# One fixed load order, a transpose moved to DMA, a gate sum in one VectorE pass and a paired epilogue in a gated sequence mixer

## The chip, the cores and the metric

The kernel runs on one NeuronCore of one Trainium2 chip. The metric is the device time of one execution in microseconds (us). The span of the profile is about 2 us shorter than that time (215.2 us against 217.1 us in the profiled run of the kernel before). Runs of one kernel mostly agree within 0.3%, but now and then one is far slower; such runs are marked slow and are compared with nothing.

Engine names in the profile: PE is TensorE (matmuls), PEld its weight loads, DVE is VectorE, ACT is ScalarE, POOL is GpSimd, SP is the engine that issues the DMAs, PEclk the clock that TensorE was granted, as a share of full speed.

## The reference

The inputs are bf16, sequence 2048, width 640, hidden width 1536.

```python
x = A_q
g = _sigmoid((x * gate_w).sum(-1, keepdims=True))
a = _A_ref(x, A_k, A_v, A_shift_k, A_ssm_k, A_ssm_D)
b = _B_ref(x, B_w1, B_b1, B_w2, B_b2)
return g * a + (1 - g) * b

def _A_ref(q, k, v, shift_k, ssm_k, ssm_D):
    # [cut] k_shift: a causal convolution of k along the sequence with 4 taps per channel
    kv = k_shift * v
    # [cut] y: a causal convolution of kv along the sequence with ssm_k (2048 taps per channel),
    #       written with a real FFT of length 4096
    y = y + kv * ssm_D[None, None, :]
    return q * y

def _B_ref(x, w1, b1, w2, b2):
    h = _layernorm(x, axis=-1)
    u = jnp.einsum("bsd,sf->bdf", h, w1) + b1             # mixes along the sequence
    u = _gelu(u)                                          # the tanh approximation
    y = jnp.einsum("bdf,fs->bds", u, w2) + b2
    return (lambda x, *d: x.transpose(*d))(y, 0, 2, 1)
```

## The kernel before

The long convolution is done in a frequency domain that is split into four interleaved parts. The names that the profile shows:

- **ssm → wT → C_82, C_83**: ssm_k is loaded, transposed on TensorE (ScalarE evicts it as wT; to evict is to copy a result from PSUM, into which TensorE writes, to SBUF, the on-chip working memory), and multiplied with the table FTB of cosines and sines ("W-forward", 128 matmuls). ScalarE evicts the result as C_82 (first half of the sequence) and C_83 (second half). VectorE then combines the four parts with two-input passes ("mixing", which also writes SS).
- **KT, DG → ksh → vkv, kv**: k is loaded transposed. The 4-tap convolution is 35 matmuls per 512 rows with DG, a set of diagonal matrices that GpSimd builds from shift_k (shk). ScalarE evicts ksh, VectorE multiplies it by v: vkv (first half), kv (second half).
- **vkv, kv with FTB → C_84, C_85**: the "A-forward", twice 64 matmuls. Then VectorE multiplies the spectra, and the inverse uses GTB, the transpose of FTB.
- **X, ring → GT → O**: x is loaded as X; layer-norm statistics (bn_stats, bn_aggr) and normalisation on VectorE; m1 (w1 in two buffers "ring", 384 matmuls); gelu on ScalarE; m2 (w2 as W_0 and W_1, 384 matmuls). None of this needs the convolution, so m1 and m2 serve as filler for TensorE.
- **gate**: the sum of x · gate_w (loaded as gwb) per row goes into gpre, tanh gives gth, and small GpSimd passes give g, 1 - g and (1 - g) · b2.

A list scheduler inside the kernel places all operations with estimated durations before anything runs. The outcome is one fixed order per engine, and each engine then works in that order: an operation whose input is late holds up everything behind it on its engine.

These are the parts that the change and the argument touch:

```python
        ssm_load(0)
        x_load(0)
        ssm_load(1)
        dma(Drow[:, :], dr(A_ssm_D, 0, [[0, 1], [1, D]]), 1280)
        dma(shk[:, :, :], dr(A_shift_k, 0, [[4, 128], [512, ND], [1, 4]]), 5120, noncontig=True)
        dma(gwb[:, :], dr(gate_w, 0, [[0, 128], [1, D]]), 128 * 1280)
        x_load(1)
        ssm_load(2)
        ssm_load(3)
        x_load(2)
        x_load(3)
        # [cut] b1, b2
        for db in range(ND):
            kT_load(0, db)
        # [cut] then, in the text, v 0/1, k second half, v 2/3, and both w1 blocks last

        def ln_apply(hk):
            # [cut]
            tt("DVE", xg[:, :, :], X[:, hk, :, :], V(gwb, 0, [[0, 4], [1, D]]), ALU.mult)
            for p in range(4):
                act(xg[:, p, :], xg[:, p, :], ACT.Copy, acc=gpre[:, 4 * hk + p:4 * hk + p + 1], name="ga")
            ts("POOL", vtmp[:, r], mv[:, r, 1], 1e-5, None, ALU.add)
            tt("POOL", rstd[:, r], vtmp[:, r], V(cst, 1, [[0, 4]]), ALU.pow)
            for p in range(4):
                # normalise X in place with mv and rstd [cut]

        tt("POOL", DG[:, :, :, :].rearrange("p a b c -> p (a b) c"),
           V(ident, 0, [[0, 20], [1, 128]]), V(shk, 0, [[1, 20], [0, 128]]), ALU.mult)
        # [cut] cast of b1 (b1f) on GpSimd
        act(gth[:, :], gpre[:, :], ACT.Tanh, scale=0.5)

        # GTB: FTB block by block through TensorE, evicted by ScalarE
        for g in range(8):
            # [cut]
            mms(vt, items, name="gtr", prio=10 ** 6 + 20 + p)
            act(GTB[:, p, :, :, :, :].rearrange("p a b c d -> p (a b c d)"), lambda s: s[:, :], ACT.Copy, vt=vt, name="gte")
```

Of the kernel before, what the change touches and what calls it, by code (L numbers as in the profile page):

```python
# [13 lines left out]
ALU = mybir.AluOpType  # L14
# [292 lines left out]
class _Op:  # L307
    __slots__ = ("eng", "dur", "emit", "prio", "idx", "ndep", "succ", "vt", "vtrole", "end", "start", "kind", "lat", "deps", "name")
# [12 lines left out]
class _Sched:  # L321
# [3 lines left out]
    def __init__(self, T, slots):  # L325
        self.T = T
        self.slots = slots
        self.ops = []
        self.hist = {}
        self.limit = {"mlp": 2}  # L330
# [20 lines left out]
    def add(self, eng, dur, emit, reads, writes, prio=None, vt=None, lat=0.0, name=""):  # L351
# [21 lines left out]
        op.deps = deps  # L373
        self._rec(op, reads, "R")
# [4 lines left out]
    def run(self):  # L379
        ops = self.ops  # L380
        for op in ops:
            op.succ = []
            op.ndep = len(op.deps)
        for op in ops:
            for d in op.deps:
                d.succ.append(op)
        engs = list(ENGS) + ["SP", "QA"]
# [18 lines left out]
        while started < n:  # L406
# [6 lines left out]
            for e in engs:  # L413
# [42 lines left out]
                if op.vt is not None:  # L456
                    op.vt.left -= 1
                    if op.vt.left == 0:
                        heapq.heappush(frees, (op.end + 0.05, op.vt.slot, op.vt.cls))
                for s in op.succ:  # L460
# [36 lines left out]
def _build(nc, A_q, A_k, A_v, A_shift_k, A_ssm_k, A_ssm_D, B_x, B_w1, B_b1, B_w2, B_b2, gate_w, out):  # L497
# [8 lines left out]
    with ExitStack() as es:  # L506
# [72 lines left out]
        xg = alloc("xg", [128, 4, D], BF16, at=base_of(GT))  # L579
# [6 lines left out]
        cgb = [alloc(f"cgb{i}", [128, D], BF16, at=base_of(FTB) + 1280 * i) for i in range(6)]  # L586
# [19 lines left out]
        def ts(eng, o, a, s1, s2, op0, op1=None, mode=1, prio=None):  # L606
            n = n_of(o)
            d = dve_dur(n, mode) if eng == "DVE" else n / 900.0 + 0.3
# [44 lines left out]
        def mms(vt, items, prio=None, name="mm"):  # L653
            dur = sum(max(n_of(r), 64) for _, _, r, _, _ in items) / 2400.0
# [10 lines left out]
        ndma = [0]  # L665

        def dma(o, i, nbytes, stream="SP", prio=None, sem=None, rate=230.0, **kw):
# [5 lines left out]
            return SC.add(stream, nbytes / rate / 1000.0, lambda s: T.dma(stream, o, i, sem, **kw), [i], [o], prio=prio, lat=-1.0, name="dma")  # L673
# [13 lines left out]
        def ssm_load(hk):  # L687
            dma(ssm[:, :, 512 * hk:512 * hk + 512], dr(A_ssm_k, 512 * hk, [[S, 128], [128 * S, ND], [1, 512]]), 128 * ND * 1024)

        def x_load(hk):  # L690
            dma(X[:, hk, :, :], dr(A_q, 512 * hk * D, [[4 * D, 128], [1, 4 * D]]), 128 * 5120)

        def w1_load(c, hk):
            dma(ring[c % 2][:, 4 * hk:4 * hk + 4, :], dr(B_w1, 512 * hk * F + 512 * c, [[4 * F, 128], [F, 4], [1, 512]]), 128 * 4096)

        def kT_load(h, db):
            dma(KT[h][:, db, 16:1040], A_k[0, 1024 * h:1024 * h + 1024, db * 128:db * 128 + 128], 128 * 2048, rate=170.0, transpose=True)

        def v_load(hk):
            dst = vkv0[:, hk, :, :] if hk < 2 else v1[:, hk - 2, :, :]  # L700
            dma(dst, dr(A_v, 512 * hk * D, [[4 * D, 128], [1, 4 * D]]), 128 * 5120)
# [4 lines left out]
        dma(Drow[:, :], dr(A_ssm_D, 0, [[0, 1], [1, D]]), 1280)  # L706
        dma(shk[:, :, :], dr(A_shift_k, 0, [[4, 128], [512, ND], [1, 4]]), 5120, noncontig=True)
        dma(gwb[:, :], dr(gate_w, 0, [[0, 128], [1, D]]), 128 * 1280)
        x_load(1)
        ssm_load(2)  # L710
        ssm_load(3)
        x_load(2)
        x_load(3)
        dma(b1t[:, :], dr(B_b1, 0, [[1, 128], [128, FT]]), 3072, noncontig=True)
        dma(b2t[:, :].rearrange("p (a b) -> p a b", a=4), dr(B_b2, 0, [[4, 128], [512, 4], [1, 4]]), 4096, noncontig=True)
# [12 lines left out]
        for p in PORD:  # L728
            pv = pint[:, p, :, 1, :]
            tt("DVE", pv, V(acol, p, [[4, 2], [0, 256]]), V(brow, 0, [[0, 2], [1, 256]]), ALU.mult, mode=1)  # L730
            ts("DVE", pint[:, p, :, 0, :], pv, 1024.0, None, ALU.add)
            pa = pint[:, p, :, :, :].rearrange("q a b c -> q (a b c)")
            ts("DVE", pa, pa, 4095, None, ALU.bitwise_and)
# [3 lines left out]
        def transp(h, p, kt):  # L737
            vt = _VT("t")
# [12 lines left out]
        def fwd(src, h, p, dst, slot, scale, name):  # L751
            for k2 in range(2):
                for c in range(2):
                    vt = _VT("f")
# [9 lines left out]
        def mixing(R, Th, Ts):  # L764
# [5 lines left out]
            tt("DVE", sl(Th, Ts), sl(R, 0), sl(R, 2), ALU.add)  # L770
            tt("DVE", sl(R, 0), sl(R, 0), sl(R, 2), ALU.subtract)
# [291 lines left out]
```

## Time and profile before

The median is 217.5 us. What matters in the profile:

| reading | value |
|---|---|
| TensorE busy | 192.9 us, 90% of the span |
| VectorE busy / ScalarE busy | 184.5 us / 119.3 us |
| end of the second A-forward | 98.1 us |
| unbroken TensorE work from | 72.95 us to 211.6 us |
| C_83 evictions end; products vkv start at | 51.0 us; 61.2 and 64.0 us |

The head of the page (busy time; then busy tenths in 40 slices of 5.4 us):

```profile
PE 192.9 (90%) x1406; PEld 139.7 (65%) x1406; DVE 184.5 (86%) x197; ACT 119.3 (55%) x181; POOL 18.0 (8%) x22
PE   0579944999879899999999999999999999999993
ACT  2798999799984996395213112113314472323751
PEclk9999995599999999999999999999999999999998
```

TensorE has gaps in the first third only, and two slices there were run at half clock (0.50 from 33.3 to 43.0 us). From the chain that ended last (start in us, duration in us, what):

```profile
19.96 9.05 ACT C_82 L641 x15
29.02 2.81 ACT xg L641 x8
34.20 2.94 ACT xg L641 x8
43.77 7.27 ACT C_83 L641 x12
51.04 2.83 ACT xg L641 x8
55.70 2.87 ACT xg L641 x8
72.95 138.65 PE pp L291 x1022
```

Until about 60 us ScalarE paces: its evictions, with the gate sums (xg) among them. After 73 us only TensorE counts, at 138.65 / 1022 = 0.136 us per matmul.

### The profile page before, as it was taken

Reading aid. Unit: us, or ns where it says so; the run is one execution under the profiler, and the core shown is the slowest. Engines: PE = TensorE matmul, PEld = TensorE weight load, DVE = VectorE, ACT = ScalarE, POOL = GpSimd, SP = SyncE. Lnnn points to the kernel's source line nnn. Section 1 sums busy time; section 2 is a strip of 40 time slices with the busy share of each in tenths; the row PEclk is TensorE's granted clock in tenths of the full one; section 3 lists DMA queues with packets and bytes.
Section 4 is the critical chain, followed back from the end, with each engine's and each line's share of the span. In section 5 each row is a group of like instructions: output and inputs, shape, how many; then the busy total and the mean of one; then the engine's idle time right before and its main releaser. Section 6 shows DMA issues by size and latency. Waiting matters only on the chain.

```text
span 215.2 us, 3363 instructions
## 1 busy us (share of the span) xinstructions
PE 192.9 (90%) x1406; PEld 139.7 (65%) x1406; DVE 184.5 (86%) x197; ACT 119.3 (55%) x181; POOL 18.0 (8%) x22
## 2 busy tenths in 40 slices
PE   0579944999879899999999999999999999999993
PEld 0456523556547557766777777778887778887672
DVE  8999599998999258966999999999997669998650
ACT  2798999799984996395213112113314472323751
POOL 1262215004060000000000000000000000000000
PEclk9999995599999999999999999999999999999998
DMA  5997999999100000000480095077070098000131
GB/s 182 355 375 149 143 176 215 349 353 412 64 0 3 0 0 3 0 0 3 128 262 3 3 318 215 3 237 299 28 265 2 3 276 261 4 0 0 61 125 62
DMA packets 32721, 28.71 MB, mean 133 GB/s; under 512 B 14145, under 2 KB 31170, under 8 KB 32706
## 3 DMA queue, kind: packets, MB, share of 16 engines
q1 hardware_dynamic: 32706, 28.49, 43.7%
q8 instruction: 11, 0.18, 0.4%
q14 instruction: 4, 0.03, 0.0%
HBM read 23.25 MB, written 2.62 MB: 120 GB/s over the span
## 4 chain that ended last, share of the span: by engine, by line
PE 72%; ACT 23%; DMA 2%; issue 0%; DVE 0%
PE pp L291 72%; ACT xg L641 5%; ACT C_82 L641 4%; ACT C_83 L641 3%; ACT wT L641 3%; DMA ssm<-in_A_ssm_k_dram 2%; ACT FTB L641 2%; ACT L641 2%; ACT ksh_94 L641 2%; ACT GTB L641 1%; ACT C_84 L641 1%; ACT ksh_95 L641 0%; ACT O_100 L641 0%; ACT GT L641 0%; DVE O_100 L603 0%
## 5 line engine op out<-in xcount | busy, mean ns | idle before, releaser
L291 PE MATMUL pp<-X,ring_80 128*128 128x320 bf16 x256 | 35.6, 299 | 1.5 <-ACT ksh_95 L641 1.5
L641 ACT ACTIVATE O_100<-pp,c_66,omg 128x640 bf16<-128x640 f32 x16 | 14.2, 885 | 35.0 <-PE pp L291 35.0
L291 PEld LDWEIGHTS pp<-X,ring_80 128*128 128x128 bf16 x256 | 24.9, 98 | 11.5 <-issue 1.8
L641 ACT ACTIVATE GT<-pp,b1f 128x640 bf16<-128x640 f32 x12 | 9.5, 793 | 38.1 <-PE pp L291 38.0
L291 PE MATMUL pp<-GT,W_1_99 128*128 128x320 bf16 x192 | 26.9, 299 | 0.0
L291 PE MATMUL pp<-GT,W_0_98 128*128 128x320 bf16 x192 | 26.4, 299 | 0.0
L291 PEld LDWEIGHTS pp<-GT,W_1_99 128*128 128x128 bf16 x192 | 21.7, 113 | 4.4
L291 PEld LDWEIGHTS pp<-GT,W_0_98 128*128 128x128 bf16 x192 | 21.8, 113 | 4.3
L291 PE MATMUL pp<-wT,FTB 128*128 128x320 bf16 x128 | 21.8, 335 | 0.0
L291 PE MATMUL pp<-ident,ssm 128*128 128x128 bf16 x80 | 9.5, 287 | 12.9 <-ACT wT L641 6.8
L291 PEld LDWEIGHTS pp<-wT,FTB 128*128 128x128 bf16 x128 | 12.4, 109 | 9.0 <-ACT C_82 L641 1.9
L291 PE MATMUL pp<-X,ring_81 128*128 128x320 bf16 x128 | 17.7, 299 | 0.0
L291 PEld LDWEIGHTS pp<-ident,ssm 128*128 128x128 bf16 x80 | 7.1, 136 | 15.1 <-ACT wT L641 8.0
L291 PEld LDWEIGHTS pp<-X,ring_81 128*128 128x128 bf16 x128 | 12.5, 98 | 4.8
L790 DVE BATCH_NORM_STATS2 stats<-X 128x6 f32<-128x320 bf16 x32 | 13.5, 461 | 0.0
L641 ACT ACTIVATE wT<-pp 128x640 bf16<-128x640 f32 x16 | 10.1, 740 | 4.5 <-PE pp L291 4.5
L603 DVE TENSOR_TENSOR C_83<-C_84 128x2560 bf16<-128x2560 bf16 x4 | 5.9, 1490 | 7.2 <-ACT C_84 L641 7.2
L641 ACT ACTIVATE xg<-xg 128x640 bf16<-128x640 bf16 x16 | 11.8, 804 | 0.0
L641 ACT ACTIVATE C_83<-pp 128x640 bf16<-128x640 f32 x16 | 10.1, 746 | 1.5 <-PE pp L291 1.5
L603 DVE TENSOR_TENSOR C_84<-C_85 128x2560 bf16<-128x2560 bf16 x5 | 7.4, 1490 | 3.8 <-ACT C_85 L641 3.8
L603 DVE TENSOR_TENSOR C_85<-C_85 128x2560 bf16<-128x2560 bf16 (+1 forms) x6 | 10.3, 1710 | 0.1
L291 PE MATMUL pp<-vkv_91,FTB 128*128 128x320 bf16 x64 | 9.7, 301 | 0.6 <-ACT GT L641 0.6
(116 smaller groups left out, 335.1 us busy)
## 6 DMA issues: line engine op xcount, KB each, us to landing
ring_80<-in_B_w_dram SPq DMA_DIRECT2D x8, 512.0 KB, 6.0
W_0_98<-in_B_w_dram SPq DMA_DIRECT2D x4, 768.0 KB, 5.8
W_1_99<-in_B_w_dram SPq DMA_DIRECT2D x4, 768.0 KB, 5.3
ssm<-in_A_ssm_k_dram SPq DMA_DIRECT2D x4, 640.0 KB, 8.5
X<-in_A_q_dram SPq DMA_DIRECT2D x4, 640.0 KB, 8.9
out_dram<-O_100 SPq DMA_DIRECT2D x16, 160.0 KB, 2.1
ring_81<-in_B_w_dram SPq DMA_DIRECT2D x4, 512.0 KB, 8.6
vkv_91<-in_A_v_dram SPq DMA_DIRECT2D x2, 640.0 KB, 10.1
```

What stands on the lines that cost most here:

```text
L291: ins = self.nc.tensor.matmul(ps_ap, lhsT=lhsT, rhs=rhs, start=start, stop=stop, skip_group_check=True)
L603: return SC.add(eng, d, lambda s: T.op(eng, lambda e: e.tensor_tensor(o, a, b, op), [a, b], [o]), [a, b], [o], prio=prio, name="tt")
L641: return T.op("ACT", lambda e: e.activation(o, src, func, **kw), rr + [src], ww)
L790: SC.add("DVE", 0.42, (lambda o, i: lambda s: T.op("DVE", lambda e: e.bn_stats(o, i), [i], [o]))(o, i), [i], [o])
```

## The change

The change has four parts. The loads are issued in one fixed order (first ssm_k and x, then the small tables, the first w1 block, k, v, the second w1 block, the rest of k and v), so that TensorE has m1 matmuls early. GTB is made by DMA transposes instead of TensorE and ScalarE. The gate sum is one VectorE pass per tile, with accumulation, instead of a product on VectorE and 16 sums on ScalarE. The epilogue works on pairs of tiles, with 8 stores instead of 16. Beside these, some durations in the scheduler's model are corrected, PSUM buffers are shared out to the stages in another way, and the mixing uses wider passes in three of its four places.

```diff
-        dma(shk[:, :, :], dr(A_shift_k, 0, [[4, 128], [512, ND], [1, 4]]), 5120, noncontig=True)
-        dma(gwb[:, :], dr(gate_w, 0, [[0, 128], [1, D]]), 128 * 1280)
-        x_load(1)
+        dma(gwb[:, :], dr(gate_w, 0, [[0, 128], [1, D]]), 128 * 1280, chain=True)
+        for hk in range(1, 4):
+            x_load(hk)
         ssm_load(2)
         ssm_load(3)
-        x_load(2)
-        x_load(3)
+        dma(shk[:, :, :], dr(A_shift_k, 0, [[4, 128], [512, ND], [1, 4]]), 5120, noncontig=True, chain=True)
+        # [cut] b1, b2
+        for hk in range(4):
+            w1_load(0, hk)
         for db in range(ND):
             kT_load(0, db)
# [cut] every load gets chain=True: it may not be issued before the one written ahead of it
+            stt("DVE", junk[1][:, :], xs, 1.0, gwb[:, :], ALU.mult, ALU.mult, acc=gpre[:, t:t + 1])
-            tt("DVE", xg[:, :, :], X[:, hk, :, :], V(gwb, 0, [[0, 4], [1, D]]), ALU.mult)
-            for p in range(4):
-                act(xg[:, p, :], xg[:, p, :], ACT.Copy, acc=gpre[:, 4 * hk + p:4 * hk + p + 1], name="ga")
-        for g in range(8):
-            # [cut] TensorE transposes and ScalarE evictions of GTB
+        for p in range(4):
+            dma(GTB[:, p, :, :, :, :].rearrange("q a b c d -> q (a b c) d"), FTB[:, p, :, :, :, :].rearrange("q a b c d -> q (a b c) d"), 128 * 2048, rate=200.0, transpose=True, prio=10 ** 5)
# inverse, per pair of tiles:
-                    tt("DVE", cg[:, :], cg[:, :], qv, ALU.mult)
-                    tt("DVE", O1[:, hk, p, :], cg[:, :], O1[:, hk, p, :], ALU.add)
-                    dma(dr(out, (512 * hk + p) * D, [[4 * D, 128], [1, D]]), O1[:, hk, p, :], 128 * 1280, sem="out")
+                tt("DVE", cg[:, :, :], cg[:, :, :], (q_lo if h == 0 else q_hi)[:, :, p, :], ALU.mult)
+                tt("DVE", ov, cg[:, :, :], ov, ALU.add)
+                dma(dr(out, (1024 * h + p) * D, [[4 * D, 128], [512 * D, 2], [1, D]]), ov, 256 * 1280, sem="out")
# [cut] model durations, PSUM slot classes, wider mixing passes
```

More of the change, by code (lines that the diff above doesn't have):

```diff
@@ L307 @@
 class _Op:
-    __slots__ = ("eng", "dur", "emit", "prio", "idx", "ndep", "succ", "vt", "vtrole", "end", "start", "kind", "lat", "deps", "name")
+    __slots__ = ("eng", "dur", "emit", "prio", "idx", "ndep", "succ", "vt", "vtrole", "end", "start", "kind", "lat", "deps", "name", "after", "nafter", "asucc")
 class _VT:
@@ L329, in __init__ @@
         self.hist = {}
-        self.limit = {"mlp": 2}
+        self.limit = {"mlp": 2, "cv": 3}
     def _conf(self, op, aps, mode, deps):
@@ L373, in add @@
         op.deps = deps
+        op.after = set()
         self._rec(op, reads, "R")
@@ L382, in run @@
             op.succ = []
-            op.ndep = len(op.deps)
+            op.asucc = []
+            op.ndep = len(op.deps) + len(op.after)
         for op in ops:
@@ L386, in run @@
                 d.succ.append(op)
+            for d in op.after:
+                d.asucc.append(op)
         engs = list(ENGS) + ["SP", "QA"]
@@ L459, in run @@
                         heapq.heappush(frees, (op.end + 0.05, op.vt.slot, op.vt.cls))
+                for s in op.asucc:
+                    avail[s] = max(avail[s], op.start)
+                    s.ndep -= 1
+                    if s.ndep == 0:
+                        heapq.heappush(pend[s.eng], (avail[s], s.prio, s.idx))
                 for s in op.succ:
@@ L578, in _build @@
         ksh = [alloc(f"ksh{i}", [128, 4, D], BF16, at=base_of(GT) + 5120 * (1 + i)) for i in range(2)]
-        xg = alloc("xg", [128, 4, D], BF16, at=base_of(GT))
         pint = alloc("pint", [128, 4, 2, 2, 256], I32, at=base_of(ring[1]))
@@ L585, in _build @@
         q_hi = alloc("q_hi", [128, 2, 4, D], BF16, at=base_of(C[0]))
-        cgb = [alloc(f"cgb{i}", [128, D], BF16, at=base_of(FTB) + 1280 * i) for i in range(6)]
+        cgb = [alloc(f"cgb{i}", [128, 2, D], BF16, at=base_of(FTB) + 2560 * i) for i in range(3)]
         def n_of(ap):
@@ L604, in tt, with ts @@
                           [a, b], [o], prio=prio, name="tt")
-        def ts(eng, o, a, s1, s2, op0, op1=None, mode=1, prio=None):
+        def ts(eng, o, a, s1, s2, op0, op1=None, mode=1, prio=None, extra=0.0):
             n = n_of(o)
-            d = dve_dur(n, mode) if eng == "DVE" else n / 900.0 + 0.3
+            d = dve_dur(n, mode) + extra if eng == "DVE" else n / 900.0 + 0.3
             rr = [a] + [x for x in (s1, s2) if isinstance(x, bass.AP)]
@@ L653, in mms @@
         def mms(vt, items, prio=None, name="mm"):
-            dur = sum(max(n_of(r), 64) for _, _, r, _, _ in items) / 2400.0
+            dur = sum(max(n_of(r) / 2400.0, 0.117) for _, _, r, _, _ in items)
             rd = []
@@ L665, in _build, with dma @@
         ndma = [0]
-        def dma(o, i, nbytes, stream="SP", prio=None, sem=None, rate=230.0, **kw):
+        last = [None]
+        def dma(o, i, nbytes, stream="SP", prio=None, sem=None, rate=280.0, chain=False, **kw):
             if sem is None:
@@ L672, in dma @@
                 T.add_dma_sem(sem, es.enter_context(nc.semaphore(f"s_{sem}")))
-            return SC.add(stream, nbytes / rate / 1000.0, lambda s: T.dma(stream, o, i, sem, **kw), [i], [o], prio=prio, lat=-1.0, name="dma")
+            o_ = SC.add(stream, nbytes / rate / 1000.0, lambda s: T.dma(stream, o, i, sem, **kw), [i], [o], prio=prio, lat=-1.0, name="dma")
+            if chain:
+                if last[0] is not None:
+                    o_.after.add(last[0])
+                last[0] = o_
+            return o_
         def dr(t, off, ap):
@@ L687, in ssm_load, with after @@
         def ssm_load(hk):
-            dma(ssm[:, :, 512 * hk:512 * hk + 512], dr(A_ssm_k, 512 * hk, [[S, 128], [128 * S, ND], [1, 512]]), 128 * ND * 1024)
+            dma(ssm[:, :, 512 * hk:512 * hk + 512], dr(A_ssm_k, 512 * hk, [[S, 128], [128 * S, ND], [1, 512]]), 128 * ND * 1024, chain=True)
         def x_load(hk):
-            dma(X[:, hk, :, :], dr(A_q, 512 * hk * D, [[4 * D, 128], [1, 4 * D]]), 128 * 5120)
+            dma(X[:, hk, :, :], dr(A_q, 512 * hk * D, [[4 * D, 128], [1, 4 * D]]), 128 * 5120, chain=True)
         def w1_load(c, hk):
-            dma(ring[c % 2][:, 4 * hk:4 * hk + 4, :], dr(B_w1, 512 * hk * F + 512 * c, [[4 * F, 128], [F, 4], [1, 512]]), 128 * 4096)
+            dma(ring[c % 2][:, 4 * hk:4 * hk + 4, :], dr(B_w1, 512 * hk * F + 512 * c, [[4 * F, 128], [F, 4], [1, 512]]), 128 * 4096, chain=True)
         def kT_load(h, db):
-            dma(KT[h][:, db, 16:1040], A_k[0, 1024 * h:1024 * h + 1024, db * 128:db * 128 + 128], 128 * 2048, rate=170.0, transpose=True)
+            dma(KT[h][:, db, 16:1040], A_k[0, 1024 * h:1024 * h + 1024, db * 128:db * 128 + 128], 128 * 2048, rate=170.0, transpose=True, chain=True)
         def v_load(hk):
             dst = vkv0[:, hk, :, :] if hk < 2 else v1[:, hk - 2, :, :]
-            dma(dst, dr(A_v, 512 * hk * D, [[4 * D, 128], [1, 4 * D]]), 128 * 5120)
+            dma(dst, dr(A_v, 512 * hk * D, [[4 * D, 128], [1, 4 * D]]), 128 * 5120, chain=True)
+        def after(o_, *prev):
+            o_.after.update(prev)
+            return o_
         ssm_load(0)
@@ L705, in _build @@
         ssm_load(1)
-        dma(Drow[:, :], dr(A_ssm_D, 0, [[0, 1], [1, D]]), 1280)
-        dma(shk[:, :, :], dr(A_shift_k, 0, [[4, 128], [512, ND], [1, 4]]), 5120, noncontig=True)
-        dma(gwb[:, :], dr(gate_w, 0, [[0, 128], [1, D]]), 128 * 1280)
-        x_load(1)
+        dma(Drow[:, :], dr(A_ssm_D, 0, [[0, 1], [1, D]]), 1280, chain=True)
+        dma(gwb[:, :], dr(gate_w, 0, [[0, 128], [1, D]]), 128 * 1280, chain=True)
+        for hk in range(1, 4):
+            x_load(hk)
         ssm_load(2)
         ssm_load(3)
-        x_load(2)
-        x_load(3)
-        dma(b1t[:, :], dr(B_b1, 0, [[1, 128], [128, FT]]), 3072, noncontig=True)
-        dma(b2t[:, :].rearrange("p (a b) -> p a b", a=4), dr(B_b2, 0, [[4, 128], [512, 4], [1, 4]]), 4096, noncontig=True)
+        dma(shk[:, :, :], dr(A_shift_k, 0, [[4, 128], [512, ND], [1, 4]]), 5120, noncontig=True, chain=True)
+        dma(b1t[:, :], dr(B_b1, 0, [[1, 128], [128, FT]]), 3072, noncontig=True, chain=True)
+        dma(b2t[:, :].rearrange("p (a b) -> p a b", a=4), dr(B_b2, 0, [[4, 128], [512, 4], [1, 4]]), 4096, noncontig=True, chain=True)
+        for hk in range(4):
+            w1_load(0, hk)
         for db in range(ND):
@@ L730, in _build @@
             tt("DVE", pv, V(acol, p, [[4, 2], [0, 256]]), V(brow, 0, [[0, 2], [1, 256]]), ALU.mult, mode=1)
-            ts("DVE", pint[:, p, :, 0, :], pv, 1024.0, None, ALU.add)
+            ts("DVE", pint[:, p, :, 0, :], pv, 1024.0, None, ALU.add, mode=2)
             pa = pint[:, p, :, :, :].rearrange("q a b c -> q (a b c)")
-            ts("DVE", pa, pa, 4095, None, ALU.bitwise_and)
+            ts("DVE", pa, pa, 4095, None, ALU.bitwise_and, mode=2)
             act(FTB[:, p, :, :, :, :].rearrange("q a b c d -> q (a b c d)"), pa, ACT.Sin, bias=cst[:, 0:1],
@@ L737, in transp @@
         def transp(h, p, kt):
-            vt = _VT("t")
+            vt = _VT("cv")
             items = []
@@ L753, in fwd @@
                 for c in range(2):
-                    vt = _VT("f")
+                    vt = _VT("cv")
                     items = []
@@ L762, in fwd, with mixing @@
                     act(o, two, ACT.Copy, vt=vt, name=name + "e", **kw)
-        def mixing(R, Th, Ts):
+        def mixing(R, Th, Ts, fine=False):
             def sl(h, s, n=1):
@@ L769, in pr @@
                 return V(h, s * SL + (1280 if rev else 0), [[-1280 if rev else 1280, 2], [1, 1280]])
-            tt("DVE", sl(Th, Ts), sl(R, 0), sl(R, 2), ALU.add)
-            tt("DVE", sl(R, 0), sl(R, 0), sl(R, 2), ALU.subtract)
-            tt("DVE", sl(Th, Ts + 1), sl(R, 1), sl(R, 3), ALU.add)
-            tt("DVE", sl(R, 1), sl(R, 1), sl(R, 3), ALU.subtract)
+            for i, n in (((0, 1), (1, 1)) if fine else ((0, 2),)):
+                tt("DVE", sl(Th, Ts + i, n), sl(R, i, n), sl(R, 2 + i, n), ALU.add)
+                tt("DVE", sl(R, i, n), sl(R, i, n), sl(R, 2 + i, n), ALU.subtract)
             tt("DVE", sl(R, 2), sl(Th, Ts), sl(Th, Ts + 1), ALU.add)
@@ L789, in ln_tile @@
                     o, i = stats[:, t, 6 * ci:6 * ci + 6], xs[:, 320 * ci:320 * ci + 320]
-                    SC.add("DVE", 0.42, (lambda o, i: lambda s: T.op("DVE", lambda e: e.bn_stats(o, i), [i], [o]))(o, i), [i], [o])
+                    SC.add("DVE", 0.46, (lambda o, i: lambda s: T.op("DVE", lambda e: e.bn_stats(o, i), [i], [o]))(o, i), [i], [o])
                 o, i = mv[:, t, :], stats[:, t, :]
                 SC.add("DVE", 0.2, (lambda o, i: lambda s: T.op("DVE", lambda e: e.bn_aggr(o, i), [i], [o]))(o, i), [i], [o])
+            stt("DVE", junk[1][:, :], xs, 1.0, gwb[:, :], ALU.mult, ALU.mult, acc=gpre[:, t:t + 1])
         def ln_apply(hk):
@@ L806, in ln_apply @@
                 t = 4 * hk + p
-                ts("DVE", X[:, hk, p, :], X[:, hk, p, :], mv[:, t, 0:1], rstd[:, t:t + 1], ALU.subtract, ALU.mult, mode=4)
+                ts("DVE", X[:, hk, p, :], X[:, hk, p, :], mv[:, t, 0:1], rstd[:, t:t + 1], ALU.subtract, ALU.mult, mode=4, extra=0.17)
         srcW = lambda h: (lambda kt, p, ci: wT[:, 2 * h + kt, p, 320 * ci:320 * ci + 320])
@@ L820, in _build @@
             if h == 0:
-                mixing(C[0], SS, 0)
+                mixing(C[0], SS, 0, fine=True)
             else:
@@ L834, in _build @@
             v_load(hk)
+        for hk in range(4):
+            w1_load(1, hk)
         for db in range(ND):
@@ L838, in _build @@
             v_load(hk)
-        for hk in range(4):
-            w1_load(0, hk)
-        for hk in range(4):
-            w1_load(1, hk)
         def v1mix(Wh, Ws, Vh, Vs):
@@ L857, in kv @@
             for d0, nb in ((0, 2), (2, 2), (4, 1)):
-                vt = _VT("k")
+                vt = _VT("cv")
                 items = []
@@ L909, in w2_load @@
                 dma(W2[hk % 2][:, 6 * a:6 * a + 6, :], dr(B_w2, a * 6 * 128 * S + 512 * hk, [[S, 128], [128 * S, 6], [1, 512]]), 128 * 6144)
-        for g in range(8):
-            vt = _VT("g")
-            items = []
-            for b in range(8 // 2):
-                pass
-            p, kt = g // 2, g % 2
-            if kt == 0:
-                continue
-            for b in range(8):
-                kt_, c_, k2_ = b // 4, (b // 2) % 2, b % 2
-                items.append(((lambda s, b=b: s[:, 128 * b:128 * b + 128]), FTB[:, p, kt_, c_, k2_, :], ident[:, :], True, True))
-            mms(vt, items, name="gtr", prio=10 ** 6 + 20 + p)
-            act(GTB[:, p, :, :, :, :].rearrange("p a b c d -> p (a b c d)"), lambda s: s[:, :], ACT.Copy, vt=vt, name="gte")
+        for p in range(4):
+            dma(GTB[:, p, :, :, :, :].rearrange("q a b c d -> q (a b c) d"), FTB[:, p, :, :, :, :].rearrange("q a b c d -> q (a b c) d"), 128 * 2048, rate=200.0, transpose=True, prio=10 ** 5)
         HORD = (2, 3, 0, 1)
@@ L993, in inverse @@
                 hz, sz = Z[p]
+                cg = cgb[ncg[0] % len(cgb)]
+                ncg[0] += 1
                 for kt in range(2):
-                    hk = 2 * h + kt
-                    t = 4 * hk + p
-                    vt = _VT("i")
+                    t = 8 * h + 4 * kt + p
+                    vt = _VT("cv")
                     items = []
@@ L1004, in inverse @@
                     mms(vt, items, name="inv")
-                    cg = cgb[ncg[0] % len(cgb)]
-                    ncg[0] += 1
-                    act(cg[:, :].rearrange("p (a b) -> p a b", a=2), two, ACT.Copy, scale=gg[:, t:t + 1], vt=vt, name="cg")
-                    qv = (q_lo if h == 0 else q_hi)[:, kt, p, :]
-                    tt("DVE", cg[:, :], cg[:, :], qv, ALU.mult)
-                    tt("DVE", O1[:, hk, p, :], cg[:, :], O1[:, hk, p, :], ALU.add)
-                    dma(dr(out, (512 * hk + p) * D, [[4 * D, 128], [1, D]]), O1[:, hk, p, :], 128 * 1280, sem="out")
+                    act(cg[:, kt, :].rearrange("p (a b) -> p a b", a=2), two, ACT.Copy, scale=gg[:, t:t + 1], vt=vt, name="cg")
+                ov = O1[:, 2 * h:2 * h + 2, p, :]
+                tt("DVE", cg[:, :, :], cg[:, :, :], (q_lo if h == 0 else q_hi)[:, :, p, :], ALU.mult)
+                tt("DVE", ov, cg[:, :, :], ov, ALU.add)
+                dma(dr(out, (1024 * h + p) * D, [[4 * D, 128], [512 * D, 2], [1, D]]), ov, 256 * 1280, sem="out")
         ncg = [0]
```

## The prediction

> **What bounds the kernel now.** The span is 215.2 us, PE busy 192.9 us (page, part 1). The chain of waits ends in 138.65 us of unbroken PE from 72.95 us on: 1022 matmuls, 135.7 ns each; only removing matmuls helps there. The loss lies before: in the stretch table PE is busy about 46 us of the first 73, and in slices 7 and 8 of the page the granted clock is 0.5. The chain there is ACT: C_82 evictions 9.05 us (0.60 each), two rounds of "xg" (29 to 38 us, PE busy 3.1 of 9.0), C_83, two more rounds of xg inside the ksh evictions (51 to 59 us).
>
> **Removed.** ACT: 16 xg passes, 0.72 us apart (four rows of the chain, 11.5 us, all before 59 us); 4 GTB evictions (4.0 us); one table load (1.28 us). PE: 32 FTB transposes (3.7 us). DVE: 4 xg products (8.9 us).
>
> **Added.** DVE: 16 scalar_tensor_tensor passes. batch_norm_stats of 320 columns starts every 0.42 us, so 640 columns[...] is an estimated 0.75 us: 12 us. DMA: 4 transposes of 256 KB. The ten k transposes took about 20 us together (DMA saturated, 145 GB/s), so about 8 us, between the k and v loads.[...]
>
> **Moved.** First w1 block ahead of the k transposes: PE gets MLP matmuls as filler by about 24 us instead of 61.6. ACT stays the pacer early: wT of half 0 done near 14 us (18.7 before), C_82 near 24 (29.0), C_83 near 38 (51.0). Then kv is PE work (0.90 us per 7 matmuls), and vkv waits on DVE: 13 statistics tiles of 1.7 us, the first mixing (11 us), and v, landed near 43 us; the A-forward starts near 50 us (68.4 before, really 73). The second A-forward finishes about 91 us (98 before).
>
> **The sum.** From there 768 matmuls x 135.7 ns = 104 us. DVE needs about 64 us to the first inverse tile, PE about 67, so DVE is just hidden. The tail grows from 1.4 to about 2.5 us before the last output DMA: one eviction, two 1280-wide DVE passes. About 91 + 104 + 5 = 200 us span, plus the 2.3 us between span and time: 202 us, 7% faster.
>
> The half clock should vanish.[...] the filler should prevent it. Worth about 3 us, within the sum.
>
> **What would show it.** Granted clock 0.9 or more throughout; no xg in ACT; C_83 evictions ending at 36 to 41 us; unbroken PE from 50 to 60 us; DVE near 100% busy until 60 us; no PE wait for GTB.
>
> **What would make it wrong.** SBUF-to-SBUF transposes much slower than those from DRAM hold back v in the same queue: up to 5 to 8 us. scalar_tensor_tensor slower than 0.75 us: each 0.1 us is 1.6 us on DVE.[...] tanh (needing all 16 gate sums) and the first gelu (needing the last normalised X) can block evictions: 1 to 3 us. More filler than I assume: 196 us.
>
> Predicted 202 us, range 196 to 209; faster 0.95, same 0.04, slower 0.01.

The sum came to 91 + 104 + 5 us of span and 2.3 us more, 202 us. The 0.75 us of a gate pass, within the 91, is the author's estimate; the trace shows the 0.42 us of a pass over 320 columns, and twice that would be 0.84. That the filler would prevent the half clock, worth about 3 us within the sum, was the author's estimate too.

## More of the kernel before

The lines of the timeline give start, duration, engine, line, operation, out<-in, size.

```profile
9.67 4.46 POOL L603 TENSOR_TENSOR DG<-ident,shk 128x2560 bf16<-128x2560 bf16 x1 [8.07 <-DMA shk<-in_A_shift_k_dram]
11.04 4.43 DVE L603 TENSOR_TENSOR xg<-X,gwb 128x2560 bf16<-128x2560 bf16 x1
32.64 1.48 DVE L603 TENSOR_TENSOR xg<-X,gwb 128x2560 bf16<-128x2560 bf16 x1
```

The same VectorE product takes 1.48 us alone and 4.43 us beside GpSimd's DG product.

## The result, and the profile after

The median after is 210.11 us (209.94 to 210.69, four runs). The ratio to the kernel before is 0.967, with a 95% interval of 0.964 to 0.970: 3.3% faster. Ratios here are the mean time of one kernel's fast runs over that of the other's of the same rounds, so they are not quite the ratio of the medians quoted. The prediction said 202 us and at most 209: the direction was right, about half of the gain did not come.

The head of the page, after:

```profile
PE 187.9 (90%) x1370; PEld 136.5 (65%) x1374; DVE 189.8 (91%) x203; ACT 104.3 (50%) x144; POOL 19.7 (9%) x22
PE   0699947999987899999999999999999999999990
ACT  4989960886378964586211112122313264413571
PEclk9999995899999999999999999999999999999999
```

ScalarE lost 15.0 us of work, TensorE 5.0 us; VectorE gained 5.3 us. Parts of the chain that ended last, after:

```profile
20.16 4.83 DVE junk_75 L629 x2
28.41 1.35 POOL vtmp L621
29.77 1.37 POOL b1f L843
31.13 1.02 POOL rstd L611
61.13 1.28 ACT L649
67.79 1.28 ACT L649
79.84 123.62 PE pp L291 x909
203.49 0.80 ACT cgb_105 L649
```

No xg is left, and ScalarE is no longer the early pacer; VectorE and the small GpSimd passes that feed it are. The two rows of 1.28 us on ScalarE are table loads, for tanh at 61 us and for gelu at 68 us. The timeline after, VectorE and GpSimd around 20 us and 28 to 34 us:

```profile
19.33 0.83 DVE L808 BATCH_NORM_STATS2 stats<-X 128x6 f32<-128x320 bf16 x2
20.08 4.91 DVE L629 SCALAR_TENSOR_TENSOR junk_75<-X,gwb 128x640 bf16<-128x640 bf16 x1
25.79 0.80 DVE L629 SCALAR_TENSOR_TENSOR junk_75<-X,gwb 128x640 bf16<-128x640 bf16 x1
...
19.84 4.46 POOL L611 TENSOR_TENSOR DG<-ident,shk 128x2560 bf16<-128x2560 bf16 x1 [2.10 <-DMA shk<-in_A_shift_k_dram]
...
28.25 2.83 DVE L611 TENSOR_TENSOR SS<-C_82 128x2560 bf16<-128x2560 bf16 x2
28.41 1.35 POOL L621 TENSOR_SCALAR vtmp<-mv 128x4 f32<-128x4 f32 x1 [4.10 <-DVE mv L810]
32.77 2.03 PE L291 MATMUL pp<-X,ring_80 128*128 128x320 bf16 x7 [4.34 <-DVE X L622]
```

One gate pass took 4.91 us instead of 0.80: it ended at 24.99 us, 0.69 us after the DG product on GpSimd (24.30). The statistics pass (one input from SBUF) that ran into the start of DG kept its 0.83 us. In the other direction, vtmp, a GpSimd pass over 4 elements per partition, took 1.35 us beside VectorE's two-input SS pass; its sister at 16.39 us took 0.24. So passes of the two engines delayed each other here, in both directions. In each of these two overlaps the pass that started second took longer, and it ended shortly after the first: the gate pass by 0.69 us, vtmp by about 0.1 us (an estimate, with half of the 2.83 us for the first SS pass). Why, the traces do not show.

The last line is TensorE waiting 4.34 us for the normalised X, which m1 matmuls that the scheduler had put ahead of the W-forward needed. Around this wait, and around one of 2.94 us for wT in the kernel before, the granted clock was low: from 29 to 38 us it is 0.73 before and 0.62 after. The table by stretch, columns from:to, length, PE, PEld, DVE, ACT, POOL (busy us and instructions), PEclk, DMA share, GB/s, first before, then after:

```profile
29.00:38.00 9.00, 3.07 (x29) 2.16 (x29) 9.00 (x13) 9.00 (x23) 4.10 (x3) 0.73 1.02 210
```

```profile
29.00:38.00 9.00, 5.23 (x21) 2.99 (x22) 7.91 (x10) 1.85 (x3) 5.37 (x4) 0.62 1.04 205
```

The milestones, all from the timelines, in us:

| | before | predicted | after |
|---|---|---|---|
| wT of the first half done | 18.7 | 14 | 14.2 |
| C_82 evictions end | 29.0 | 24 | 23.8 |
| C_83 evictions end | 51.0 | 38 | 46.0 |
| products vkv, first and second start | 61.2, 64.0 | – | 50.2, 54.6 |
| first A-forward starts | 68.4 | 50 | 56.9 |
| second A-forward ends | 98.1 | 91 | 97.8 |
| m1, m2 and inverse matmuls left then | 832 | 768 | 776 |
| last matmul ends | 211.6 | 195 | 203.5 |
| span | 215.2 | 200 | 208.6 |

Up to 24 us the prediction held, and then 7 to 8 us were lost once and for all. The second A-forward ends hardly earlier than before. Nearly all of the gain comes from the 56 more m1 matmuls that TensorE has done by then (56 × 0.136 = 7.6 us), less 1.5 us of longer tail (208.6 - 203.5 = 5.1 us, before 215.2 - 211.6 = 3.6 us).

Where the first A-forward comes from, in the timeline after (the second vkv product, then the first matmuls that read vkv):

```profile
54.59 1.49 DVE L611 TENSOR_TENSOR vkv_91<-ksh_95,vkv_91 128x2560 bf16<-128x2560 bf16 x1
56.90 1.25 PE L291 MATMUL pp<-vkv_91,FTB 128*128 128x320 bf16 x8
```

The product ends at 56.08 us, 0.8 us before TensorE needs it. From 32.77 us, when X has come, to 56.90 TensorE has no gap over 0.2 us: it works off the W-forward, ksh and 24 m1 matmuls, until 37.7 us at half clock (0.50). So VectorE's lateness reaches the A-forward by two ways that come out almost together: through X and TensorE's backlog, and through the vkv products. To take away one of the two is therefore not enough (e1b, below).

### The profile page after: what moved, and what is told of

Its sections match the earlier page's. It is cut to its first block, busy times and chain, and to the rows that moved or that the text cites. A ratio compares the mean times of both kernels' runs of the same rounds, so it can differ in the third digit from the quotient of the medians.

```text
span 208.6 us, 3251 instructions
## 1 busy us (share of the span) xinstructions
PE 187.9 (90%) x1370; PEld 136.5 (65%) x1374; DVE 189.8 (91%) x203; ACT 104.3 (50%) x144; POOL 19.7 (9%) x22
## 4 chain that ended last, share of the span: by engine, by line
PE 78%; DVE 9%; ACT 4%; DMA 4%; POOL 2%; SPq 1%; issue 1%
PE pp L291 78%; DVE junk_75 L629 5%; DMA gwb<-in_gate_w_dram 4%; DVE stats L808 2%; ACT C_84 L649 2%; ACT L649 1%; DVE X L622 1%; SPq L265 1%; POOL b1f L843 1%; POOL vtmp L621 1%; POOL rstd L611 0%; DVE mv L810 0%; DVE cgb_105 L611 0%; DVE O_99 L611 0%; ACT cgb_105 L649 0%
## 5 line engine op out<-in xcount | busy, mean ns | idle before, releaser
L291 PE MATMUL pp<-X,ring_80 128*128 128x320 bf16 x256 | 37.9, 304 | 4.3 <-DVE X L622 4.3
L291 PE MATMUL pp<-wT,FTB 128*128 128x320 bf16 x128 | 20.6, 319 | 0.1
L629 DVE SCALAR_TENSOR_TENSOR junk_75<-X,gwb 128x640 bf16<-128x640 bf16 x16 | 17.0, 1064 | 2.0 <-DMA gwb<-in_gate_w_dram 2.0
L291 PE MATMUL pp<-X,ring_81 128*128 128x320 bf16 x128 | 17.6, 299 | 0.0
L291 PEld LDWEIGHTS pp<-wT,FTB 128*128 128x128 bf16 x128 | 11.6, 104 | 8.8 <-ACT C_82 L649 2.1
L291 PE MATMUL pp<-ident,ssm 128*128 128x128 bf16 x80 | 8.5, 266 | 7.9 <-DMA ssm<-in_A_ssm_k_dram 7.2
L649 ACT ACTIVATE C_83<-pp 128x640 bf16<-128x640 f32 x16 | 10.0, 757 | 7.3 <-PE pp L291 7.3
L291 PEld LDWEIGHTS pp<-ident,ssm 128*128 128x128 bf16 x80 | 6.5, 128 | 10.2 <-DMA ssm<-in_A_ssm_k_dram 7.5
L291 PE MATMUL pp<-vkv_91,FTB 128*128 128x320 bf16 x64 | 10.4, 300 | 2.8 <-ACT C_84 L649 2.1
L649 ACT ACTIVATE C_85<-pp 128x640 bf16<-128x640 f32 x16 | 10.1, 709 | 5.4 <-PE pp L291 5.4
L649 ACT ACTIVATE C_84<-pp 128x640 bf16<-128x640 f32 x16 | 10.3, 700 | 4.7 <-PE pp L291 4.7
L611 DVE TENSOR_TENSOR C_84<-C_85 128x2560 bf16<-128x2560 bf16 (+1 forms) x4 | 7.2, 1821 | 3.5 <-ACT C_85 L649 3.5
```

The lines of the kernel that those rows point to most:

```text
L291: ins = self.nc.tensor.matmul(ps_ap, lhsT=lhsT, rhs=rhs, start=start, stop=stop, skip_group_check=True)
L611: return SC.add(eng, d, lambda s: T.op(eng, lambda e: e.tensor_tensor(o, a, b, op), [a, b], [o]), [a, b], [o], prio=prio, name="tt")
L629: eng, lambda e: e.scalar_tensor_tensor(out=o, in0=a, scalar=sc, in1=b, op0=op0, op1=op1, accum_out=acc),
L649: return T.op("ACT", lambda e: e.activation(o, src, func, **kw), rr + [src], ww)
```

## The experiments

Two explanations stood at first, and the texts use these letters:

- **A, VectorE paces.** Up to the vkv products VectorE is full. A gate pass takes about 4 us longer beside DG, and the wait for gwb wastes 2 us more. TensorE's stall at 28 to 33 us costs nothing of its own.
- **B, the filler.** Eight m1 matmuls stand ahead of the W-forward in TensorE's fixed order, wait 4.3 us for X, and with this wait and the half clock (0.50 from 31.0 to 37.7 us) delay C_83 and all that follows.

Where a later text uses another letter for a theory, the paragraph behind it says in plain words what was tested. All kernels except e2 and e3 are built to compute the reference's result in full; those two hold wrong diagonals in DG.

In the first, second and fourth group the fixed order of every engine is kept as it is after the change (in e11, as it is in u2), and only the named operations are moved in it. In the third group a part of the change is undone and the scheduler makes its order anew.

### First group: DG beside VectorE, and the filler (kernel before in the same rounds: 216.99 us)

**e1_late_filler.** The filler behind the W-forward:

```diff
         SC.run()
+        m = [x for x in SC.ops if x.name == "m1"][1]          # 8 matmuls
+        SC.order.remove(m)
+        k = max(i for i, x in enumerate(SC.order) if x.name == "W" and x.eng == "PE")
+        SC.order.insert(k + 1, m)
         SC.emit()
```

> Only the 8 filler matmuls of the first w1 block's second quarter move on PE, from ahead of the half-1 forward of w to behind it; every other queue keeps its order. Theory A (VectorE paces the stretch up to vkv, and PE's stall at 28 to 33 us only stands in for it): the 4.3 us PE wait and the half clock at 31 to 37 us go, the C_83 evictions end near 39 us instead of 46, but the first vkv product still starts at 49 to 50 us and the time stays within 1.5 us of 210.1. Theory B (the stall of the in-order PE queue and the cold clock after it are the loss): 203 to 206 us.

210.66 us, ratio 0.970 [0.967, 0.972]: no change against the kernel after (0.967). The edit was run once more as e1b, below.

**e2_dg_memset.** DG is filled by a GpSimd memset, which has no input. This tests whether GpSimd's DG product is what made the gate pass beside it 4.1 us longer:

```diff
-        tt("POOL", DG[...], V(ident, ...), V(shk, ...), ALU.mult)
+        SC.add("POOL", 2560 / 500.0 + 0.3, lambda s: T.op("POOL", lambda e: e.memset(DG[:, :, :, :], 0.05), [], [DG[:, :, :, :]]), ...)
```

> DG is filled by a constant on GpSimd instead of the product of two SBUF tensors, so the kv part is wrong on purpose; all orders are kept. Theory A[...]: the pass of 4.91 us falls to about 0.8, X of the second quarter is normalised near 28 us, PE's wait shrinks below 1 us, the vkv product starts near 46 us, 205 to 207 us. Rival C (the gate pass is simply too slow on VectorE): one pass stays far above 0.8 us and the time stays at 209 to 210.5.

207.35 us, ratio 0.955 [0.953, 0.957]. No gate pass took over 0.81 us any more. But the memset met another VectorE pass (the normalisation of X, start and duration as above):

```profile
17.88 2.23 POOL L842 MEMSET DG<- 128x2560 bf16 x1
17.96 3.39 DVE L622 TENSOR_SCALAR X<-X,mv,rstd 128x640 bf16<-128x640 bf16 x4
```

These four passes take 1.52 us elsewhere, so VectorE lost 1.9 us here and gained only about 2 net. TensorE's wait for X fell from 4.3 to 1.4 us, and the time fell by about 2.6 us (0.967 - 0.955 of 217 us). The output check passed in spite of the wrong DG (presumably because the part of the output that depends on it is small in this data), so that check does not guard the DG values. This gain is not that of the shorter gate pass alone: with the wait for X down to 1.4 us there is no half clock either (granted clock 1.00 from 20 to 200 us, also in e3).

**e3_both.** Both edits.

> Both edits of the two runs before (wrong result on purpose). Theory A: no more than 1 us better than the constant DG alone, 204.5 to 206.5 us. Theory B: the gains add, 201 to 203 us.

207.21 us, ratio 0.955 [0.953, 0.957]. Moving the filler as well is worth 0.1 us.

**e4_dg_dve.** DG made by VectorE itself, in the time in which it waits for gwb. shk is loaded right behind the first block of x. The result passed the check, which, as e2 shows, would not notice a wrong DG; the product is the same one on another engine.

```diff
-        tt("POOL", DG[...], V(ident, ...), V(shk, ...), ALU.mult)
+        SC.add("POOL", ..., lambda s: T.op("DVE", lambda e: e.tensor_tensor(dgo, dga, dgb, ALU.mult), [dga, dgb], [dgo]), [dga, dgb], [dgo], name="dg")
+        SC.order.remove(shk_op)                     # after SC.run()
+        SC.order.insert(SC.order.index(x0_op) + 1, shk_op)
+        # the "dg" operation goes ahead of the first gate pass
```

> A correct version: shk is loaded right after the first x block and VectorE itself makes DG[...] in the 2 us in which it waits for gwb anyway; orders otherwise kept. Theory A: VectorE is some 3 us earlier from 25 us on, no pass above 1 us, 206 to 208 us. Theory C: 209 to 211 us.

206.02 us in its fast runs, ratio 0.949 [0.947, 0.951]: about 4 us less than after. The lines are shown from e6, which has the same edit. DG takes 2.77 us on VectorE, and the gate passes follow without a wait:

```profile
8.96 2.77 DVE L844 TENSOR_TENSOR DG<-ident,shk 128x2560 bf16<-128x2560 bf16 x1
11.65 0.82 DVE L629 SCALAR_TENSOR_TENSOR junk<-X,gwb 128x640 bf16<-128x640 bf16 x1
```

So A says what was lost: half of the missing 8 us is the gate pass of 4.91 us beside DG, together with the wait that could have hidden DG, and with TensorE's stall for the late X and the half clock that came with it.

### Second group: what is left (kernel before: 217.3 us)

**e1b_late_filler.** The edit of e1 once more, for a clean profile.

> The late-filler kernel again, for a trace in the fast state (its first profile fell in a slow one). Theory A: no PE wait at 28 to 33 us, granted clock near 1.0 from 29 to 38 us, C_83 evictions ending near 39 us, yet the first vkv product starting at 49 to 50 us as in the changed kernel, about 210 us.

211.77 us in one run (state unknown, but the profile is undisturbed). The stall at 28 to 33 us is gone and the C_83 evictions end at 39.9 us, 6 us earlier. It was all for nothing: vkv starts at 49.98 and 54.41 us as in the kernel after (50.16 and 54.59). TensorE now waits at a later place, and the half clock is there too. TensorE in the timeline of e1b around 52 us:

```profile
51.96 6.18 PE L291 MATMUL pp<-X,ring 128*128 128x320 bf16 x24 [3.24 <-DVE X L622]
57.97 1.25 PE L291 MATMUL pp<-vkv,FTB 128*128 128x320 bf16 x8
```

Twenty-four matmuls in 6.18 us is 0.26 us each, about twice the usual; after the change the same 24 take 3.42 us. The granted clock is 0.50 from 50.8 to 57.6 us here, and in the kernel after from 31.0 to 37.7 us. So the clock was 0.50 in or shortly after a wait of 3.24 us here, of 4.34 us in the kernel after and of 2.94 us in the kernel before (there from 33.3 us, the wait ends at 32.48). In u2, where TensorE's longest wait after that for the first ssm_k load is 1.9 us, it was 1.00 from 20 to 200 us. What sets the clock, these runs do not show further. B falls as far as the place of the filler goes: moving it gains nothing here, and 0.1 us where no half clock is left in either kernel (e3 against e2). What the half clock costs e1b cannot say, because it only moved; other runs can (see the clock, below).

**e6_tanh_late.** e4, and tanh with the three small passes behind it is moved behind the last gelu.

```diff
+        g4 = [x for x in SC.ops if x.name in ("gth", "gg", "omg", "c2")]
+        # [cut] remove them from the order
+        k = max(i for i, x in enumerate(SC.order) if x.name == "gelu")
+        SC.order[k + 1:k + 1] = g4
```

> The version with DG on VectorE, and tanh with the three small GpSimd passes behind it moved after the last gelu on ScalarE and GpSimd. Theory D (ScalarE's in-order stop for tanh, a table load of 1.28 us and the wait for all 16 gate sums, holds the A-forward's evictions): the PE waits for C_84 fall from 2.1 to below 1 us, one table load less, 204.3 to 205.3 us against 206.0. Rival (that stop is hidden by VectorE's later work): 205.7 to 206.3.

204.80 us (204.79 to 204.81), ratio 0.943 [0.940, 0.946]. This is the fastest kernel: 5.7% under before, about 2.5% under after. ScalarE has one table load less. Its table loads are, in the kernel after and then in e6:

```profile
61.13 1.28 ACT L649 ACT_TABLE_LOAD   x1
67.79 1.28 ACT L649 ACT_TABLE_LOAD   x1
```

```profile
61.90 1.28 ACT L649 ACT_TABLE_LOAD   x1
```

(each has one more at the start, so three in all against two). In e6 the tanh right behind the last gelu, at 128.5 us, has none; the result passed the check, but whether that check would notice a wrong gate was not tried. In the kernel after, the load at 67.79 us cost nothing beyond its 1.28 us that shows: the eviction at 67.07 us lasts 0.70, and the gelu follows at 69.08. TensorE's waits for the A-forward's evictions fell from 2.1 to 1.0 us. The waits of TensorE (waited for: us in total, times, longest), after and e6, where the tile C_84 is called C:

```profile
PE pp L291 <- DMA ssm<-in_A_ssm_k_dram: 7.2, 2, 5.6
PE pp L291 <- DVE X L622: 4.3, 1, 4.3
PE pp L291 <- ACT C_84 L649: 2.1, 4, 1.4
```

```profile
PE pp L291 <- DMA ssm<-in_A_ssm_k_dram: 8.0, 2, 5.6
PE pp L291 <- ACT C L649: 1.0, 5, 0.3
...
PE pp L291 <- DVE X L622: 0.5, 2, 0.3
```

In e6 the C_83 evictions end at 40.4 us, vkv starts at 46.50 and 50.93 us, the first A-forward at 51.92 us, the second A-forward ends at 91.9 us and the last matmul at 197.6 us. These are the predicted milestones within 2.6 us. The same two lines as for the kernel after, in e6:

```profile
50.93 1.48 DVE L611 TENSOR_TENSOR vkv<-ksh,vkv 128x2560 bf16<-128x2560 bf16 x1
51.92 1.53 PE L291 MATMUL pp<-vkv,FTB 128*128 128x320 bf16 x8
```

Here TensorE begins the A-forward before the second product has ended (52.41 us) and has to wait for it within the first eight matmuls: VectorE sets the date.

**e7_vkv_first.** e4, with one tile of statistics and gate sum moved from ahead of each of the first two vkv products to behind it, so that the products come earlier.

> The version with DG on VectorE, and one statistics tile (1.6 us of VectorE) moved from ahead to behind of each of the first two vkv products. Theory A (VectorE paces the start of the A-forward): the A-forward starts 1 to 2 us earlier, 204.3 to 205.3 us. If kv on PE or the landing of v paces it: 205.7 to 206.3.

205.80 us, ratio 0.948 [0.945, 0.950]: 0.2 us under e4. The first product did come earlier, at 45.15 us, but not the second, and the A-forward did not either (51.91 us). The lines show passes of VectorE and GpSimd beside each other again:

```profile
45.15 1.49 DVE L611 TENSOR_TENSOR vkv<-ksh,vkv 128x2560 bf16<-128x2560 bf16 x1
45.19 1.54 POOL L621 TENSOR_SCALAR vtmp<-mv 128x4 f32<-128x4 f32 x1 [9.29 <-DVE mv L811]
47.89 1.52 DVE L622 TENSOR_SCALAR X<-X,mv,rstd 128x640 bf16<-128x640 bf16 x4 [1.24 <-POOL rstd L611]
```

vtmp took 1.54 us beside the product, against 0.24 alone, so X was normalised no earlier than in e6 (47.90 us), and the 24 m1 matmuls that stand ahead of the A-forward in TensorE's order need this X.

**e8_both.** e6 and e7 together.

> Both edits. If both theories hold and add, 202.8 to 204.3 us, which would be the time predicted for the change; if VectorE is late again at the second A-forward, 204 to 205.

205.37 us, ratio 0.946 [0.943, 0.948], 0.6 us worse than e6 alone. Late tanh, worth 1.2 us on e4, is worth 0.4 us on e7. An order that is better by VectorE alone is not better for the whole.

### Third group: one part of the change undone (kernel before: 217.25 us)

Here the code of one part is taken from the kernel before, and the rest is as after.

**u1_gate_old.** The gate sum by a product on VectorE and sums on ScalarE.

> The changed kernel with the old gate sum (product on VectorE, sum on ScalarE); the static order is made anew by the same list scheduler. Theory A (the changed kernel is paced by VectorE up to 57 us, ScalarE has room): undoing costs little, 209 to 213 us. If the saved ScalarE time is what the change gained: 214 us or more.

214.62 us, ratio 0.988 [0.986, 0.990]. In this setting the new gate sum is worth about 4.5 us, more than A expected (the other line of the expectation, 214 us or more, came true): ScalarE paces again, and TensorE waits 9.4 us for wT.

**u2_gtb_old.** GTB by TensorE and ScalarE.

> The changed kernel with the inverse table transposed on PE and evicted by ScalarE as before. My estimate: 3.7 us of PE and 4 us of ScalarE come back, but 6 us of DMA before v go; 210 to 214 us.

208.09 us, ratio 0.959 [0.955, 0.963]. Undoing this part wins 2 us. The trace shows that the scheduler made another order, with no filler ahead of the W-forward. A gate pass of 4.2 us beside DG is there all the same. Whether the DMA transposes cost time is tested by e9, below.

**u3_loads_old.** The load order of before.

> The changed kernel with the old load order (w1 after all k transposes, v last, shk early, no fixed chain). If the early filler is the gain of the change: 213 us or more. With shk early the GpSimd product lies elsewhere and X is normalised earlier, so theory A allows 208 to 212 us.

215.89 us, ratio 0.994 [0.992, 0.996]. In this setting the load order is worth 5.8 us, again more than A allowed (the line for the early filler, 213 us or more, came true). TensorE waits 4.1 us for w1 and has less filler early. Part of the 5.8 us comes late and from the new order: at 194 us TensorE waits 3.2 us for VectorE (a tile C), and the 32 matmuls behind it take 7.32 us. DG comes at 9.7 us here, and a gate pass beside it took 4.0 us: the long gate pass does not need the moved load of shk, it costs 3.2 us here against 4.1.

**u4_epi_old.** The epilogue of single tiles, with 16 stores.

> The changed kernel with single 640-column passes and 16 output stores. The tail after the last matmul should be shorter by 0.8 to 1.5 us and VectorE busier by about 1 us before it: 208.5 to 210 us.

210.53 us, ratio 0.969 [0.965, 0.973], against 0.967: the paired epilogue is worth nothing that can be measured.

The parts do not add up to the whole: undoing u1 or u3 alone gives back most of the gain. As the waits of TensorE suggest, each of them brings back one of two things that both have to go: ScalarE's load, or the lack of early m1 work.

### Fourth group: the rest (kernel before: 217.23 us)

**e9_gtb_late.** The kernel after, with the four GTB transposes issued behind the last v load.

> The changed kernel with only the four transposes of the inverse table moved behind the last v load in the DMA queue; all other orders kept. If their DMA time ahead of v is what the run with the table on PE won back: v lands some 6 us earlier and the time is 207.5 to 208.7 us. If that win came from another static order: v and k wait for nobody, the vkv products start when VectorE is ready as before, 209.5 to 210.7 us.

210.06 us, ratio 0.966 [0.963, 0.970]: no change. v was issued 5 us earlier (33.76 against 38.78 us) and vkv started when it did before (50.08 and 54.51 us). So the transposes cost nothing here. That leaves, for the 2 us that u2 won, its other order, with no half clock in the profiled run (1.00 from 20 to 200 us). This is by elimination and was not tested by itself.

**e10_norm_first.** e6, with the small GpSimd passes moved away from the SS passes: X is normalised ahead of the two-input SS passes, and the cast of b1 stands behind rstd. The load of shk stands one block later than in e6. This tests whether the slow GpSimd passes at 25 to 29 us cost time (theory E in the text): in e6, beside the two-input SS passes, vtmp takes 1.35 us and the cast 1.41, against 0.24 and 0.19 elsewhere.

> The best version so far (DG on VectorE, tanh late) with X of the second quarter normalised ahead of the first two mixing passes, its statistics neighbours in the gap, and the small cast behind rstd on GpSimd; shk behind the second ssm block. Theory E[...]: VectorE's wait for rstd falls from 2.3 to about 1.3 us, X ready near 26.5 instead of 28.7 us, 203.3 to 204.3 us. If VectorE's total work paces regardless: 204.3 to 205.

204.99 us, ratio 0.944 [0.942, 0.946]: no gain. The second block of X was normalised 2.0 us earlier (26.69 against 28.71 us) and vkv started as before (46.62 and 51.06 us). VectorE does the same passes in another sequence, and only their sum counts.

**e11_u2_fixed.** u2, with DG on VectorE as in e4 and tanh late as in e6 (shk's load one block later, as in e10).

> The version with the inverse table on PE (208.1 us) with DG on VectorE and tanh late. If the two fixes are worth the 5.3 us here that they are worth in the changed kernel: 202.5 to 203.8 us. If the k transposes, for which PE waits 2.5 us there, or kv then pace it: 204 to 206.5.

207.09 us, ratio 0.954 [0.951, 0.957], only 1.0 us better than u2, where A would have given about 5. In that order the A-forward starts at 52.69 us, later than in e6, and TensorE has new waits late in the kernel (1.7 us for the evictions O). A cure measured in one fixed order does not carry its worth into another.

## Why the prediction was wrong

**The step that failed** is this one, in the prediction's words: "C_83 near 38 … vkv waits on DVE: 13 statistics tiles of 1.7 us, the first mixing (11 us), and v, landed near 43 us; the A-forward starts near 50 us". The mechanism was right: VectorE's work sets the start of the A-forward. The sum for VectorE was too small. It left out how long a two-input VectorE pass takes beside GpSimd's DG product (4.91 us for a pass of 0.80), and that VectorE would stand still for 2.0 us waiting for gwb: together 6.1 us. It also left out that late work of VectorE comes to TensorE through X, with a wait of 4.34 us and a clock of 0.50 from 31.0 to 37.7 us, so that C_83 ended at 46.0 us and not near 38. The A-forward started at 56.9 us, and the 6.9 us by which it was late went through to the end. The sign was in the trace before: an xg product of 4.43 us beside DG, the others 1.48. The delay beside DG was thus not new (2.95 us before the change, 3.2 us in u3 with the old load order); while ScalarE paced, it did not show.

How the 8.1 us between 202 and 210.1 us divide, as the runs show it:

- about 4 us: the gate pass beside DG and the unused wait for gwb, with what they bring on TensorE (the kernel after against e4). In e6 the second vkv product starts 3.7 us earlier than in the kernel after and the A-forward 5.0 us earlier; the 1.3 us between is TensorE's backlog, half clock included;
- 1.2 us: tanh and its table load in the middle of the A-forward's evictions (e4 against e6; 0.4 us between e7 and e8, so the worth depends on the order). The prediction named this as a danger of 1 to 3 us, outside its sum;
- about 2.8 us are left in e6. Of these 1.6 us lie in the last part: 776 matmuls were left there too, not 768, and they took 105.6 us (91.9 to 197.6) instead of 104. Another 0.9 us is the second A-forward, which ends at 91.9 us instead of 91; the rest is tail and rounding. Why the first A-forward starts at 51.9 us instead of 50 is not settled: e7, e8 and e10 tried to bring it forward without success. VectorE's work up to there and the 24 filler matmuls that need the last X but one are what it waits for; which order would serve both better was not found.

**Wrong, at a cost of about 1 us (an estimate from the pairs below): the clock.** "The half clock should vanish" failed: the granted clock was 0.62 from 29 to 38 us. The filler that was to prevent it waited itself, 4.34 us for X. No experiment changed the clock alone (in e1b the half clock only moved), but runs of one and the same kernel differ in it, and the time goes with it. Of the kernel after, the run with a mean clock of 0.983 took 210.69 us and the three with 0.989 to 0.991 took 209.94 to 210.18. Of e9, the run with 0.994 took 208.70 us and the three with 0.989 to 0.991 took 209.99 to 210.16. Of u2, the run with 1.000 took 207.64 us and the one with 0.981 took 209.64. Each of these pairs rests on a single run at one end. The cost is part of the 4 us above, not in addition to them.

**Wrong in part: what VectorE does.** "DVE near 100% busy until 60 us" held only from 32 us on (the wait for gwb, and 1.1 us for rstd, lie before). The estimate of 0.75 us for a gate pass was right in itself: passes follow each other 0.73 us apart. The mean of 1.06 us over all 16 comes from the one of 4.91 us.

**Right.** ScalarE is relieved early (wT 14.2 and C_82 23.8 us against 14 and 24). The DMA transposes do not delay anything (no wait for GTB; e9). The last part is 776 matmuls at 0.136 us, 105.6 us against the 104 predicted for 768 (1.6 us too few), and the tail is 5.1 us against 5. Each GTB transpose of 256 KB landed 3.4 us (median) after its issue.

The paired epilogue took no part in the sum, beyond a longer tail, and no run shows a gain from it (u4).

## What to carry to other kernels

Cost a pass together with what runs beside it: here a two-input VectorE pass of 0.80 us took 4.01 us (u3) and 4.91 us (the kernel after) beside one GpSimd product, so this put 3 to 4 us on VectorE, which counts once VectorE paces. A fill on GpSimd, which has no input, was no escape: in e2 it met the normalising passes, and they took 3.39 us instead of 1.52. Where the orders are fixed in advance, removing a stall gains nothing if another engine sets nearly the same date (e1b), and a part of a change can only be judged with the orders pinned, because the scheduler answers every edit with a new order (u2 against e9). Look for a place where an activation function needs no table load: tanh behind the last gelu saved one of 1.28 us, and 1.2 us of the time (e6 against e4).
